# An attention and feed-forward block on one core: LayerNorm's normalisation and most of its reciprocal roots on GpSimd, GpSimd's additions without a window, and new build parameters and seeds

## The chip, the cores and the metric

The kernel runs on one core of a Trainium2 chip. The metric is the device time of one execution in microseconds; 2048 rows, bfloat16 inputs and output, one launch. The engines are TensorE (PE in the profile; PEld is its weight load), ScalarE (ACT), VectorE (DVE), GpSimd (POOL) and SyncE (SP), which here issues all DMAs.

## The reference, cut to what matters

```python
S, D, H, Dh, F = 2048, 640, 32, 20, 1536
xn = (x - mean(x)) / sqrt(var(x) + 1e-5)          # LayerNorm without weights
q = xn @ wq                                       # 32 heads of 20
k, v = xn @ wk, xn @ wv                           # one head for K and V, shared by all
p = softmax(q @ k.T * Dh ** -0.5)                 # 2048 x 2048 for each head
attn = concat_heads(p @ v) @ wo
ffn = relu(xn @ w1 + b1) ** 2 @ w2 + b2
out = x + attn + ffn
```

## The kernel before, in words

**A planner writes the order.** The kernel has no loops on the chip. While it is built, a scheduler (class `Sched`, `run` from line 292) plays the whole program through in simulated time: each part of the work is a generator that yields a request (`Req`) with an engine, a planned duration, its dependencies and a priority; the scheduler takes for each engine the request that can start first (the lowest priority number among those within 15 ns) and appends it to that engine's list. The lists are then emitted in this order, with a semaphore wait wherever an instruction depends on another engine. Each engine runs its list strictly in order, so the plan fixes who stands behind whom. Planned durations and thresholds are constants of the file. `PLAN` is a table of 64 rows, one for each half block of the attention: thresholds and, in most rows, a `seed` that flips some of the planner's choices (`pick`). Other seeds give another order of the same work.

**The opening.** x is 16 tiles of 128 rows, in chunks of four. Chunk 0 takes a short cut that computes its Q, K and V from the raw x, so that the attention can begin early. For all tiles VectorE computes mean and variance (`stats`, L708 and L711). `rst` (line 716) makes the reciprocal root on ScalarE, as a logarithm and an exponential, for half a chunk at a time in chunk 0 and for a chunk at a time in chunks 1 to 3 (L717, L723). `nmean` (L733) makes -mean x root, and `xnorm` (L743) the normalised tile on VectorE: `x * rstd + nmr`, written into the buffer `big`. The normalised tile is then transposed into `xnT`: by TensorE with an eviction by VectorE for the tiles in `PET` = 5, 6, 7 (`u_T`, L951 and L905), by a DMA transpose that SyncE issues for all others (`turn`, L910). Chunk 0 is normalised last: `X0W` = 12 makes it wait for the transposes of tiles 4 to 11. From `xnT` follow K and V of chunks 1 to 3 (`u_KT`, `u_V`; evictions L986 and L1003; a cast of V on GpSimd, L1010), the Q projections (L1053 evicts them, L1071 spreads them by DMA into `qT`) and the feed-forward. W1's load (`weights`, L655) waits until all transposes are issued, and the feed-forward until all are done, because its buffer shares memory with the normalised tiles. TensorE fills gaps of the opening with useless matmuls to keep its clock up (L1813, L1815).

**The attention** has 32 blocks (4 chunks of 512 queries x 8 groups of 4 heads), each with 16 tiles of 128 keys. Scores are computed transposed (keys on partitions, 512 queries): four heads can run at once in four row strips of TensorE, and a batch (L1318) has two, three or four of them. Each tile of keys has one of two ways:

- *A tile*: ScalarE's exponential (L1595) takes two or three heads in one instruction from adjacent PSUM banks (banks 0, 1, 2 or banks 3, 4) into one of `RING` slots. P x V is one group of four matmuls (L1896, `PT,vx`).
- *D tile*: VectorE makes the exponential from the bits of the scores: one eviction per head (L1694, `S_P1`) into one of `NPB` buffers, and then three shifted copies, the phases, which are additions of a constant to 128 x 2048 16-bit integers: on VectorE (L1715, `S_PH` and `S_STEAL`) or on GpSimd as 64-bit additions (L1777, `S_PHP`). P x V takes four groups (`pbx,vx` once, `pbx,vp` three times). Scores of D heads go to banks 5, 6, 7, which P x V and all other work share, or to bank 2 when the planner takes it from a three-head exponential: it does so when VectorE has less planned work left than `W32` ns (`poll_s`, line 1376).

`DPH` is the share of phases that VectorE takes at once; the rest go into a queue for GpSimd, out of which VectorE takes one when the queue is longer than `PHQ`.

**VectorE and GpSimd take turns.** Requests with `port=True` (VectorE's normalisation, phases L1715, squares L1106, products L1957) and all of GpSimd's work are planned so as not to overlap. GpSimd's phase additions are `under=True`: the planner puts them only beneath a VectorE instruction of at least 550 ns that is no port operation (`beneath`, line 386), and cuts them into pieces that fit there (`cut`, `pieces`). A GpSimd piece waits for the last port operation of VectorE; VectorE's port operations have no wait on GpSimd.

**The end.** The output of a tile half (128 rows x 320 columns) is W2's 12 groups of four matmuls plus Wo's six (L962). In the last chunk `u_P1` does W2's part and the ready Wo groups early and keeps the sum in SBUF (L1220), and `u_PF` does the missing Wo groups at the end, added by VectorE (L1156). `NPX` = 1 tile (two halves) is done wholly at the end by `u_PX`, and evicted by VectorE or ScalarE as a copy (L1153, L1154). The last block is normalised by `norm_last` (L1977 to L1989) on VectorE, in two halves.

## Time and profile before

| what | value |
|---|---|
| median of 3 runs | 679.76 us (679.63 to 681.91) |
| the profiled execution | 681.03 us, its span 679.3 us |
| granted clock of TensorE | 0.997 |
| instructions | 23577 |
| first and last exponential (L1595) start at | 10.9 and 669.3 us |
| DMA transposes of normalised tiles (L910) | 13 |
| D tiles (matmuls `pbx,vx` 620 / 4) | 155 of 512 |

The span runs from the first to the last instruction of that execution. Busy time of TensorE counts overlapping matmuls once, and their ends are modelled. In an order of time an instruction's line shows its start, its length, the engine, the line of the program and, in brackets, how long the engine was idle before it and who released it. L962 and L1896 are lines of helpers that many parts use; there the names of the tiles tell the parts apart.

### The profile page before, as it was taken

Reading aid. Unit: us, or ns where it says so; the run is one execution under the profiler, and the core shown is the slowest. Engines: PE = TensorE matmul, PEld = TensorE weight load, DVE = VectorE, ACT = ScalarE, POOL = GpSimd, SP = SyncE. Lnnn points to the kernel's source line nnn. Section 1 sums busy time; section 2 is a strip of 40 time slices with the busy share of each in tenths; the row PEclk is TensorE's granted clock in tenths of the full one; section 3 lists DMA queues with packets and bytes.
Section 4 is the critical chain, followed back from the end, with each engine's and each line's share of the span. In section 5 each row is a group of like instructions: output and inputs, shape, how many; then the busy total and the mean of one; then the engine's idle time right before and its main releaser. Section 6 shows DMA issues by size and latency. Waiting matters only on the chain.

```text
span 679.3 us, 23577 instructions
## 1 busy us (share of the span) xinstructions
PE 668.8 (98%) x9953; PEld 226.4 (33%) x9953; DVE 607.0 (89%) x1097; ACT 659.5 (97%) x664; POOL 452.2 (67%) x827
## 2 busy tenths in 40 slices
PE   8999999999999999999999999999999999999998
PEld 5322222233223333332223333333222333333434
DVE  7978999999999998989999888888999899997895
ACT  6989999999999999999999999999999999999995
POOL 2073775787577866777778886786666877687700
PEclk9989999999999999999999999999999999999999
DMA  7282244111110111111000112111110011111001
GB/s 222 51 145 76 56 113 102 29 22 28 30 21 16 43 42 23 47 42 26 20 20 18 28 46 46 26 34 42 30 25 18 20 39 37 32 42 47 12 2 41
DMA packets 39891, 29.90 MB, mean 44 GB/s; under 512 B 23562, under 2 KB 34795, under 8 KB 39787
## 3 DMA queue, kind: packets, MB, share of 16 engines
q1 hardware_dynamic: 39787, 28.39, 18.0%
q8 instruction: 80, 1.31, 0.8%
q14 instruction: 24, 0.20, 0.1%
HBM read 11.12 MB, written 2.62 MB: 20 GB/s over the span
## 4 chain that ended last, share of the span: by engine, by line
PE 64%; ACT 33%; DVE 2%; DMA 1%; issue 0%; POOL 0%; DVEq 0%
ACT PT L1595 32%; PE ps L1896 25%; PE ps L1318 20%; PE ps L962 19%; DMA xnT<-big 1%; DVE pbx L1694 1%; DMA pbx<-in_A_x_dram 0%; DVE stats L708 0%; PE ps L999 0%; DVE out_sb L1156 0%; PE ps L1813 0%; DVE OTs L1957 0%; DVE pbx L1715 0%; POOL pbx L1777 0%; DVE mv L711 0%
## 5 line engine op out<-in xcount | busy, mean ns | idle before, releaser
L1595 ACT ACTIVATE PT<-ps 128x1024 bf16<-128x1024 f32 (+1 forms) x642 | 653.0, 1189 | 7.1 <-PE ps L1318 6.7
L1777 POOL INT64_ADD pbx<-pbx x803 | 447.3, 576 | 171.4 <-DVE pbx L1715 74.9
L1694 DVE TENSOR_SCALAR pbx<-ps 128x512 int16<-128x512 f32 x619 | 407.0, 684 | 49.9 <-PE ps L1318 45.9
L1318 PE MATMUL ps<-qT,kT 20*128 20x512 bf16 x2048 | 250.0, 385 | 2.5 <-ACT PT L1595 2.2
L1896 PE MATMUL ps<-pbx,vp 128*32 128x512 bf16 x1860 | 169.7, 383 | 0.2
L1318 PEld LDWEIGHTS ps<-qT,kT 20*128 20x128 bf16 x2048 | 62.6, 91 | 242.4 <-ACT PT L1595 164.8
L1896 PE MATMUL ps<-PT,vx 128*32 128x512 bf16 x1428 | 136.2, 384 | 0.4 <-ACT PT L1595 0.3
L962 PE MATMUL ps<-w_sb,big 128*32 128x320 bf16 x1536 | 74.7, 302 | 0.0
L962 PE MATMUL ps<-xnT,w_sb 128*32 128x512 bf16 x960 | 73.7, 383 | 0.1
L1715 DVE TENSOR_SCALAR pbx<-pbx 128x2048 int16<-128x2048 int16 x98 | 66.5, 691 | 0.5
L1896 PEld LDWEIGHTS ps<-pbx,vp 128*32 128x32 bf16 x1860 | 45.5, 95 | 51.6 <-issue 30.6
L1896 PE MATMUL ps<-pbx,vx 128*32 128x512 bf16 x620 | 60.5, 385 | 0.1
L1896 PEld LDWEIGHTS ps<-PT,vx 128*32 128x32 bf16 x1428 | 36.1, 95 | 43.9 <-issue 31.4
L962 PEld LDWEIGHTS ps<-w_sb,big 128*32 128x32 bf16 x1536 | 32.7, 95 | 28.4 <-issue 22.0
L1098 DVE TENSOR_SCALAR hT_tmp<-ps,b1col 128x512 bf16<-128x512 f32 x48 | 35.6, 742 | 1.2 <-PE ps L962 0.9
L962 PE MATMUL ps<-wo_p,OTp 120*32 120x320 bf16 (+1 forms) x640 | 31.8, 301 | 0.1
L962 PE MATMUL ps<-xnT,wq_sb 128*32 128x512 bf16 x375 | 28.5, 383 | 0.0
L962 PEld LDWEIGHTS ps<-xnT,w_sb 128*32 128x32 bf16 x960 | 18.6, 95 | 27.3 <-issue 17.7
L1896 PEld LDWEIGHTS ps<-pbx,vx 128*32 128x32 bf16 x620 | 16.2, 95 | 18.7 <-issue 12.0
L1941 DVE COPY Tn<-ps 128x512 f32<-128x512 f32 x29 | 19.8, 682 | 0.5 <-PE ps L1896 0.5
L1106 DVE TENSOR_TENSOR big<-hT_tmp 128x512 bf16<-128x512 bf16 x48 | 20.2, 425 | 0.0
L962 PEld LDWEIGHTS ps<-wo_p,OTp 120*32 120x32 bf16 (+1 forms) x640 | 14.7, 95 | 11.6 <-issue 4.7
(95 smaller groups left out, 188.9 us busy)
## 6 DMA issues: line engine op xcount, KB each, us to landing
Rb<-kT SPq DMA_DIRECT2D x29, 256.0 KB
xres<-in_A_x_dram SPq DMA_DIRECT2D x16, 160.0 KB
out_dram<-out_sb SPq DMA_DIRECT2D x16, 160.0 KB
qT<-qpk SPq DMA_DIRECT2D x105, 20.0 KB
pbx<-in_A_x_dram SPq DMA_DIRECT2D x3, 640.0 KB
w_sb<-in_B_w_dram SPq DMA_DIRECT2D x1, 1920.0 KB
w_sb<-in_B_w_dram SPq DMA_DIRECT2D x4, 480.0 KB
OTp<-OTs SPq DMA_DIRECT2D x96, 20.0 KB
```

The costliest lines, as they stand in the source:

```text
L962: return lambda e: e.matmul(ps[32 * j:32 * j + m, b_[0], 0:n], Lj, R, start=first, stop=last, tile_position=(0, 32 * j))
L1098: v = yield Req(("dve", 658.0, 742.0, [lambda e: e.tensor_scalar(out=hT_tmp[:, k, :], in0=ps[:, b_[0], :], scalar1=b1col[:, f:f + 1], scal ...
L1106: w = yield Req(("dve", SQ_D, SQ_D + 82.0, [lambda e: e.tensor_tensor(out=h2T[:, qc % 2, f, :], in0=hT_tmp[:, k, :], in1=hT_tmp[:, k, :], ...
L1318: ins.append(lambda e, i=i, b=b, t=t, h=h: e.matmul(ps[:, i, :], kT[32 * h:32 * h + DH, t * 128:(t + 1) * 128], qT[32 * h:32 * h + DH, b % ...
L1595: op = yield Req(("act", d_, d_ + 107.0, [lambda e, slot=slot, n=n, src=src: e.activation(out=PT[:, slot:slot + n, :], in_=ps[:, src, :], ...
L1694: return Req(("dve", d_, d_ + 82.0, [lambda e: e.tensor_scalar(out=PB[:, k, hsl, :], in0=ps[:, bk:bk + np_, :], scalar1=OFFS, scalar2=0.0, ...
L1715: return Req(("dve", 600.0, 684.0, [lambda e: e.tensor_scalar(out=PB[:, k, :, :], in0=PB[:, s, :, :], scalar1=PH_D[j], scalar2=None, op0=A ...
L1777: return lambda e: e.int64_add(PB8[:, k, c0 // 4:c1 // 4], PB8[:, s, c0 // 4:c1 // 4], int(PH_D[j]) * 0x0001000100010001)
L1896: ins = [(lambda e, h=h, first=first, last=last: e.matmul(ps[32 * h:32 * h + 32, bk, :], lhs, rhs[h], start=first, stop=last, tile_positio ...
L1941: v = yield Req(("dve", 600.0, 682.0, [lambda e: e.tensor_copy(out=Tn[:, tb, :], in_=ps[:, pvb, :])]), (lambda: None if oldt() is None els ...
```

## The change

- **Normalisation and roots.** GpSimd loads library 0 behind its memsets, and library 1 (with the 64-bit addition) again when all 16 tiles are normalised; no phase addition is planned on GpSimd before that. All 16 normalisations are GpSimd's (`XPOOL`). For tiles 4 to 15 GpSimd also makes the reciprocal root, tile by tile: `var + EPS`, then that to the power -0.5, and the normalisation is `(x - mean) * rstd`. Chunk 0 keeps ScalarE's roots.
- **Transposes.** `PET` becomes 4, 5, 6, 7, 11. `X0W` = 0: chunk 0 is normalised as soon as it may; its transposes are planned after tile 11 is normalised. DMA transposes come first among what SyncE may issue.
- **GpSimd's additions** (`PUN` = False) are planned at any time, whole, and no longer beneath a VectorE instruction. Where a port operation of VectorE and a GpSimd addition or normalisation follow each other, the later waits for the earlier, in both directions.
- **Parameters**: `RING` 25 to 23, `NPB` 10 to 11, `NQS` (slots of `qT`) 6 to 4; in nearly all rows of `PLAN` `W32` 2000 to 650, `DPH` 0.3 to 0, `PHQ` 4 to 8; other seeds.
- **The end**: `NPX` = 0, all eight halves of the last chunk go through `u_P1` and `u_PF`; `PAT` 27.6 to 26.5 (the block at which `u_P1` begins); `u_PF` may begin before `u_P1`'s eviction, its groups but the last have priority 0.6 and the last one -1.
- The other lines (`spot`, `where`, `pvres`, the condition in `PVblk`) leave the planner's choices as they were with the constants given (`PVK` = 1, `PVS` = 1, `PVG` = 0).

```diff
-RING = 25
-NPB = 10
+RING = 23
+NPB = 11
...
-NQS = 6
+NQS = 4
...
-PAT = 27.6
+PAT = 26.5
...
-    (640, 3500.0, 600.0, 6000.0, 0, 900.0, 12, 2, 0.0, 3, 60.0, 600, 4.0, 2000.0, 2, 0.3, 0, 0.0, 0.0, 4, 0.5, 2, (0, 3, 400.0, 300.0), 1, 0, 8, 1.0, 2.0, 2, 99, 2000.0, -1, 400.0, 600.0),
...
+    (640, 3500.0, 600.0, 6000.0, 0, 900.0, 12, 2, 0.0, 3, 60.0, 600, 4.0, 650.0, 2, 0.0, 0, 0.0, 0.0, 8, 0.5, 2, (0, 3, 400.0, 300.0), 1, 0, 8, 1.0, 2.0, 2, 99, 2000.0, -1, 400.0, 600.0),
...
-NPX = 1
+NPX = 0
+PUN = False
+PFA, PFB, PFE = 0.6, -1.0, 0
+PVK, PVR, PVS, PVG = 1, 16, 1, 0
...
-PET = (5, 6, 7)
+PET = (4, 5, 6, 7, 11)
...
-XPOOL = ()
-X0W = 12
+XPOOL, VPOOL, LIBD = (0, 1, 2, 3, 4, 5, 6, 7, 8, 9, 10, 11, 12, 13, 14, 15), (), 5800.0
+GPW, PWD = 1, 130.0
+XG, TG = '', 'X11'
+TEDP = -1
+X0W = 0
...
+            if not PUN and self.last_port is not None and (eng == "pool" and rr.name == "PHP" or rr.port) and self.last_port.eng != eng:
+                deps = deps + [self.last_port]
...
-            if eng == "dve" and rr.port:
+            if rr.port or not PUN and rr.name == "PHP":
                 self.last_port = op
...
+            if XPOOL:
+                done["mhalf"] = yield ms(mhalf[:], -0.5, 100.0, "mhalf")
+                done["lib0"] = yield Req(("pool", 7850.0, 7850.0, [lambda e: e.load_library(library_config.all_libraries[0])]), [], -2, "lib0")
+                yield Until(lambda: have(*[f"X{st}" for st in XPOOL]) and (not VPOOL or have(*[f"VP{c}" for c in VPOOL])))
+                done["lib1"] = yield Req(("pool", LIBD, LIBD, [lambda e: e.load_library(library_config.all_libraries[1])]), [], -2, "lib1")
...
+        def rpow(st):
+            yield Until(lambda: have("lib0"))
+            v = yield (lambda: Req(("pool", PWD, PWD + 60.0, [lambda e: e.tensor_scalar(out=vtmp[:, st:st + 1], in0=mv[:, st, 1:2], scalar1=EPS, scalar2=None, op0=ALU.add)]),
+                                   (lambda: get(f"S{st}")), soon(st) - 0.3, f"RV{st}"))
+            op = yield (lambda: Req(("pool", PWD, PWD + 60.0, [lambda e: e.tensor_tensor(out=rstd[:, st:st + 1], in0=vtmp[:, st:st + 1], in1=mhalf[:, :], op=ALU.pow)]),
+                                    (lambda: get("mhalf") + [v]), soon(st) - 0.4, f"RW{st}"))
+            done[f"RW{st}"] = op
...
             if st in XPOOL:
-                alts = [("pool", 700.0, 760.0, alts[0][3])]
+                alts = [("pool", 870.0, 930.0, alts[0][3])]
+            if st in XPOOL:
+                yield Until(lambda: have("lib0"))
+            if GPW and c:
+                eng, d_, l_ = ("pool", 870.0, 930.0) if st in XPOOL else ("dve", 400.0, 440.0)
+                alts = [(eng, d_, l_, [lambda e: e.tensor_scalar(out=xn_sb[:, st, :], in0=x_sb[:, st, :], scalar1=mv[:, st, 0:1], scalar2=rstd[:, st:st + 1], op0=ALU.subtract, op1=ALU.mult)])]
+                yield Until(lambda: have(f"RW{st}"))
...
-            yield Until(lambda: f"X{st}" in done)
+            yield Until(lambda: f"X{st}" in done and (st > 3 or not TG or TG in done))
...
                 def poll():
+                    if XPOOL and "lib1" not in done:
+                        return None
...
-                    c1 = cut(2048, F_, E_)
+                    c1 = cut(2048, F_, E_) if PUN else 2048
...
-                    return Req(("pool", d_, d_ + 60.0, [part(0, c1, k, s, j)]), [acc[-1]] + pbres[k].last, 2 if left_ns(b) > PHU else -1, "PHP", under=True)
+                    return Req(("pool", d_, d_ + 60.0, [part(0, c1, k, s, j)]), [acc[-1]] + pbres[k].last, 2 if left_ns(b) > PHU else -1, "PHP", under=PUN)
```

## The prediction

> **What bounds the kernel now.** I read the page's totals first, then the table by stage, then the instructions in order of time for the stages that are not full, then the groups by shape for durations. Columns of the stage table: stage, its length, busy time of PE, PEld, DVE, ACT and POOL, granted clock, DMA share, GB/s.
>
> ```profile
> PE 668.8 (98%) x9953; PEld 226.4 (33%) x9953; DVE 607.0 (89%) x1097; ACT 659.5 (97%) x664; POOL 452.2 (67%) x827
> ```
> ```profile
> 20.00:30.00 10.00, 8.74 (x121) 3.06 (x123) 9.82 (x34) 9.14 (x12) 0.25 (x1) 1.00 0.17 34
> 30.00:40.00 10.00, 9.70 (x134) 2.89 (x126) 9.85 (x28) 9.16 (x12) 4.53 (x10) 1.00 0.61 101
> 40.00:60.00 20.00, 18.69 (x227) 5.29 (x223) 12.69 (x23) 17.58 (x20) 13.77 (x29) 0.91 0.63 139
> 60.00:100.00 40.00, 40.00 (x526) 11.09 (x526) 39.67 (x71) 40.00 (x44) 25.16 (x42) 1.00 0.30 77
> 500.00:600.00 100.00, 99.98 (x1523) 32.85 (x1520) 91.93 (x156) 99.92 (x101) 72.43 (x131) 1.00 0.13 30
> 670.00:680.00 10.00, 5.91 (x164) 3.98 (x156) 5.43 (x15) 0.85 (x2) 0.00 (x0) 0.93 0.21 69
> ```
>
> From 60 us to the last exponential ScalarE and TensorE are both full; VectorE and GpSimd are not. So a saving on VectorE or GpSimd there is worth nothing by itself. It pays only where it lets TensorE or ScalarE do less, and those two are coupled: a tile taken from ScalarE goes to VectorE and costs TensorE three more groups. What is visibly unused lies in the opening. Its ScalarE, its transposes and the chain of waits:
>
> ```profile
> 27.05 5.12 ACT L1595 ACTIVATE PT<-ps 128x1536 bf16<-128x1536 f32 x5 [0.83 <-PE ps L1318]
> ...
> 38.66 9.21 ACT L1595 ACTIVATE PT<-ps 128x1536 bf16<-128x1536 f32 x9 [0.84 <-PE ps L1318]
> 49.73 1.02 ACT L1595 ACTIVATE PT<-ps 128x1024 bf16<-128x1024 f32 x1 [1.86 <-PE ps L1318]
> 51.24 11.72 ACT L1595 ACTIVATE PT<-ps 128x1024 bf16<-128x1024 f32 x12 [0.48 <-PE ps L1318]
> ```
> ```profile
> 26.71 9.77 SPq L910 DMA_TRANSPOSE xnT<-big  x6
> ```
> ```profile
> 35.21 10.50 SPq L910 DMA_TRANSPOSE xnT<-big  x7
> 45.75 0.59 SPq L655 DMA_DIRECT2D w_sb<-in_B_w_dram  x1
> ```
> ```profile
> 41.82 5.03 DMA xnT<-big
> ```
>
> Each ScalarE gap (bracket: length, releaser) ends with a scores batch that had to wait for the next chunk of K: chunk 1 before 27, chunk 2 before 38.7, chunk 3 before 49.7. Together 0.83 + 0.84 + 1.86 + 0.48 = 4.0 us. The last chunk waits for SyncE's transposes: 12 of them, one behind the other, from 26.71 to 45.75, 1.59 us each; the chain shows that transfer for 5.03 us. W1's load is queued behind them, at 45.75.
>
> **The change, part by part.** Durations are those of one profiled execution: span 679.3, 681.03 with the 1.73 us around it, which is 1.27 above the median of 679.76. I subtract savings from the median.
>
> *Normalisation and roots off VectorE and ScalarE.*
>
> ```profile
> L717 ACT ACTIVATE vtmp<-mv 128x4 f32<-128x4 f32 x3 | 0.7, 248 | 0.0
> L723 ACT ACTIVATE rstd<-vtmp 128x4 f32<-128x4 f32 x3 | 0.6, 216 | 0.0
> L672 POOL MEMSET wo_p<- 128x640 bf16 x1 | 0.6, 631 | 0.0
> L1813 PE MATMUL ps<-kT,zeros 128*32 128x512 bf16 x76 | 6.8, 385 | 0.0
> ```
> ```profile
> L743 DVE TENSOR_SCALAR big<-pbx,rstd,nmr x16: 431/439/445, 17.4 to 36.8; 128x640 bf16<-128x640 bf16 x16
> ```
> ```profile
> 16.67 0.25 POOL L1010 CAST vx<-out_sb 128x80 bf16<-128x80 f32 x1 [11.93 <-DVE out_sb L824]
> ```
>
> VectorE loses 16 x 0.439 = 7.0 us, ScalarE six small operations, 1.3 us. GpSimd gets 16 normalisations and 12 pairs of tiny operations. No row has a GpSimd normalisation; the nearest is its 128x640 memset, 0.63 us, which reads nothing. The planner charges 0.87 and 0.13 for a tiny one, and I take those: 16 x 0.87 + 24 x 0.13 = 17 us. They fit: GpSimd is idle for 11.93 us before 16.67, and the first library load (planned at 7.85) lies in that hole, ending near 12.6 if it starts at 4.8. Tiles 4 to 7 are then normalised by 12.6 + 4 x 1.13 = 17.1, while VectorE only begins them at 17.4 now. For tiles 8 to 15 the statistics, not GpSimd, set the pace. I reckon the last normalisation near 31 (the last starts at 36.8 now) and, after the second load of 5.8, GpSimd's first addition near 38 (33.2 now, below). That delay costs nothing as long as VectorE's shares wait in buffers.
>
> The Trainium skill (GPSIMD Engine Reference, When to use GPSIMD) says that ordinary elementwise work belongs on the Vector engine, GpSimd being about half as fast for two inputs and near line rate for one. By it the move is a loss of engine time, and 0.439 against 0.63 or more agrees; but the loss falls on an idle engine. The same page (Architecture, Instruction dispatch) gives about 6 us, with no visible instruction, for the first call into a freshly loaded library. Two of them would make 12 where the planner has 13.65, so the sum would not move. No run so far shows it.
>
> *Transposes.* Tiles 4 and 11 move from SyncE to TensorE, X0W = 0 lets chunk 0 be normalised early, and chunk 3 no longer queues at the end of a full line. 11 x 1.59 = 17.5 us of transposes starting near 19, with holes, end near 38 instead of 45.75. K3 then comes near 42 (38 and the 4.0 from 45.75 to 49.73), before ScalarE needs it at 49.73 - 1.86 - 0.83 - 0.84 = 46.2, and W1's load goes out near 38, eight us earlier. So I remove the four gaps (4.0) and the roots (1.3): **ScalarE gains 5.3 us**, bounds 0 and 5.3.
>
> TensorE has to gain as well. In the opening it runs 19 filler groups (76 / 4) of 0.22, 4.1 us, idles 1.26 + 0.30 + 1.31 between 20 and 60, and loses 20 x 0.09 = 1.8 to the clock of 0.91 after the stall: 8.8 in all. Only what starts before W1 arrives can fill it (the Q projections of chunk 0, then the feed-forward): **I take 5**, bounds 0 and 8.8.
>
> *How two slacks become time.* A tile costs ScalarE 4 x 0.457 = 1.83 us (653.0 over the 498 x 2 + 144 x 3 = 1428 heads below). Given to VectorE it costs TensorE three groups of 0.22, 0.65 us. If ScalarE has A and TensorE S to spare, both end together when the time falls by 0.26 A + 0.74 S. So 0.26 x 5.3 + 0.74 x 5 = **5.1 us**.
>
> *Additions at any time, new parameters and seeds.*
>
> ```profile
> L1595 ACT ACTIVATE PT<-ps 128x1024 bf16<-128x1024 f32 x498 | 482.0, 1096 | 5.3 <-PE ps L1318 5.0
> L1777 POOL INT64_ADD pbx<-pbx x803 | 447.3, 576 | 171.4 <-DVE pbx L1715 74.9 <-DVE big L1106 30.2 <-DVE pbx L1694 23.7
> L1595 ACT ACTIVATE PT<-ps 128x1536 bf16<-128x1536 f32 x144 | 216.6, 1513 | 1.8 <-PE ps L1318 1.7
> L1896 PE MATMUL ps<-pbx,vp 128*32 128x512 bf16 x1860 | 169.7, 383 | 0.2
> L1715 DVE TENSOR_SCALAR pbx<-pbx 128x2048 int16<-128x2048 int16 x98 | 66.5, 691 | 0.5
> ```
> ```profile
> L1777 POOL INT64_ADD pbx<-pbx x803: 263/572/1048, 33.2 to 645.6; - x161
> ```
> ```profile
> L1595 ACT ACTIVATE PT<-ps 128x1024 bf16<-128x1024 f32 (+1 forms) x642 | 653.0, 1189 | 7.1 <-PE ps L1318 6.7
> ```
>
> There are 1860 / 4 = 465 phase additions: 98 on VectorE, 367 on GpSimd in 803 pieces, 1.22 us each. Whole they should cost the longest piece, 1.048 (second row: min, median, max). All 465 on GpSimd take 487 us of the 612 between 38 and 650: they fit. VectorE sheds up to 66.5. The price is mutual exclusion: about 77 remaining port operations of VectorE (48 squares, 29 normalisations of the output) wait up to 1.05 for an addition, half on average, 40 us. Behind one in VectorE's queue stand the evictions that free the PSUM banks of the scores. VectorE has 72 us idle plus the 66.5, so it has cover; I cost this at nothing, and at 40 us of VectorE without cover.
>
> What can pay is the scores batch. TensorE's order of time shows its price:
>
> ```profile
> 657.03 0.40 PE L1896 MATMUL ps<-pbx,vp 128*32 128x512 bf16 x4
> 657.25 0.39 PE L1896 MATMUL ps<-PT,vx 128*32 128x512 bf16 x4
> ...
> 658.40 0.39 PE L1318 MATMUL ps<-qT,kT 20*128 20x512 bf16 x3
> 658.72 0.73 PE L962 MATMUL ps<-w_sb,big 128*32 128x320 bf16 x16
> 659.38 0.39 PE L1318 MATMUL ps<-qT,kT 20*128 20x512 bf16 x3
> 659.70 0.59 PE L962 MATMUL ps<-w_sb,big 128*32 128x320 bf16 x12
> 660.22 0.39 PE L1318 MATMUL ps<-qT,kT 20*128 20x512 bf16 x3
> ```
>
> A group of four 512-column matmuls takes 0.22 (657.03 to 657.25), one of 320 columns 0.14 (0.66 less 0.52), so a batch with its two changes of mode takes 0.98 - 4 x 0.14 = 0.43 us, whether two, three or four heads ride in it. Each exponential has a batch, so 642. W32 falls from 2000 to 650: bank 2 is taken from a three-head exponential only when VectorE has less work left, which favours threes. But VectorE's counted work falls too, as no phases wait in it, and that favours twos. Neither end can be excluded: 680 batches (10% threes) to 621 (30%). I take 10 fewer, since VectorE's relief frees the banks sooner: 4.3 us of TensorE, x 0.74 = **3.2 us**. RING, NPB and NQS trade the same memory; I cost them at nothing while Q lands in time.
>
> *The end.*
>
> ```profile
> 670.83 1.80 PE L962 MATMUL ps<-w_sb,big 128*32 128x320 bf16 x48
> ```
> ```profile
> 672.50 0.77 DVE L1989 STREAM_TRANSPOSE OT<-qpk 128x256 bf16<-128x256 bf16 x2
> 673.50 0.49 DVE L1153 CAST out_sb<-ps 128x320 bf16<-128x320 f32 x1 [0.24 <-PE ps L962]
> 674.19 2.65 DVE L1156 TENSOR_TENSOR out_sb<-ps,w_sb 128x320 bf16<-128x320 f32 x6 [0.19 <-PE ps L962]
> ```
>
> NPX = 0 takes the 12 groups at 670.83 out of the shadow of VectorE's last normalisation and puts them into the full stretch: 1.8 x 0.74 = 1.3 lost. PF's early groups now fill the shadow and the eight additions start at once, but all eight are VectorE's: 8 x 0.44 = 3.5 from about 673.1 ends at 676.6, against 674.19 + 2.65 = 676.84 now, 0.2 back. **Net 1.1 us slower.**
>
> **Sum:** 5.1 + 3.2 - 1.1 = 7.2; 679.76 - 7.2 = **672.6 us**.
>
> **Rivals.** *Only the opening pays*: batches stay at 642; 679.76 - 5.1 + 1.1 = 675.8. For it: W32 and the counted work cancel. *Threes become common*: 621 batches, 21 x 0.43 x 0.74 = 6.7; 679.76 - 5.1 + 1.1 - 6.7 = 669.1. *The opening's gain doesn't come*: the loads take longer than planned, or the casts of V (the row at 16.67 is one) stand behind the second load and the ring of 23 fills; K1, due at 27.05 - 0.83 = 26.2 and reckoned near 21 (17.1 and some 4 for a transpose, its eviction, the projection and K's eviction), has 5 us of margin, and past it each us is lost on both engines. Then 3.2 - 1.1 remain, less a us or two: 679. *Fewer threes (slower)*: VectorE, relieved, asks for scores more often, takes bank 2, and the exponentials fall to pairs. Each batch more is two threes less and costs 0.32 us; the opening and the end give 4.0, so it decides from 642 + 13 = 655 batches (118 threes). At 668 (92 threes): 26 x 0.32 - 4.0 = 4.3 slower, 684.1. Against it: ScalarE's bank 2 was already contested at W32 = 2000.
>
> **How the numbers follow.** Forecast 0.45, only the opening 0.20, common threes 0.12, no opening gain 0.10, fewer threes 0.13. A measurement here tells about 0.5%, 3.4 us, from no change. Faster than 676.4: the forecast, the common threes and three quarters of the second case, 0.72; within: 0.13; slower: 0.15. The range, 665 to 684, takes in TensorE's whole slack of 8.8 beside common threes (669.1 less 0.74 x 3.8 = 666.3) at one end and the slower case's middle at the other.
>
> **What would show it.** As expected: no ScalarE gap over 0.5 us between 20 and 52, W1's issue before 40, TensorE's filler groups halved, the longest addition and the mean one both near 1.05, fewer than 642 exponentials.
>
> ```profile
> PEld ps L1896 <- POOL pbx L1777: 6.5, 25, 0.5
> ```
>
> Wrong: a ScalarE gap behind chunk 1 of K (library), more than 655 exponentials, TensorE waiting for GpSimd's additions (6.5 us in 25 waits now, row above), or VectorE's evictions late behind port operations.

## The result, and the profile after

The kernel after takes 707.9 us (707.2 to 712.7, 4 executions) against 680.1 us for the kernel before on the same chip: ratio 1.042 [1.037, 1.047], slower. The profiled execution took 708.4 us, its span is 706.6 us.

The page's totals and its row of granted clock (40 slices of 17.7 us):

```profile
PE 686.4 (97%) x9964; PEld 229.1 (32%) x9964; DVE 576.5 (82%) x1013; ACT 654.7 (93%) x651; POOL 519.1 (73%) x527
...
PEclk9555799999999999999999999999999999999999
```

The table by stage (columns as in the prediction):

```profile
20.00:30.00 10.00, 5.30 (x39) 2.21 (x43) 2.80 (x9) 3.02 (x4) 9.99 (x10) 0.55 0.00 0
30.00:40.00 10.00, 9.73 (x83) 2.10 (x75) 6.24 (x21) 6.86 (x7) 10.00 (x10) 0.50 0.18 35
40.00:60.00 20.00, 16.32 (x130) 3.65 (x130) 8.92 (x21) 11.18 (x12) 17.53 (x17) 0.50 0.47 75
60.00:100.00 40.00, 39.97 (x422) 9.63 (x418) 24.79 (x45) 32.74 (x35) 22.41 (x23) 0.76 0.24 76
500.00:600.00 100.00, 99.79 (x1435) 30.68 (x1435) 89.45 (x151) 99.88 (x99) 77.43 (x76) 1.00 0.13 27
```

GpSimd, nearly idle in the opening before (0.25 of 10 us from 20 to 30), is now the full engine to 58 us; ScalarE is busy for 30, 69 and 56% of the first three stages, against 91, 92 and 88% before; and TensorE runs at half its clock from 21 to 79 us. From 100 to 600 us nothing has become slower. How far behind the kernel is can be read by counting the score matmuls up to 100 us and from there to 600 (some records may be missing). Before, then after:

```profile
0.00:100.00 100.00, 33.76 (x251) 8.37 (x251) 0.98 0.46 112
100.00:600.00 500.00, 192.04 (x1596) 48.26 (x1596) 1.00 0.15 33
```
```profile
0.00:100.00 100.00, 30.66 (x165) 6.17 (x165) 0.71 0.34 87
100.00:600.00 500.00, 192.12 (x1614) 48.37 (x1611) 1.00 0.15 35
```

It is 86 matmuls behind at 100 us; at 1596 / 500 = 3.19 a us that is 27 us, the whole difference of the spans (27.3). So the loss is made in the opening. (From 100 to 600 us it does 18 score matmuls more than before; what that lead is worth is seen below, in e14.) GpSimd's groups by shape:

```profile
L777 POOL TENSOR_SCALAR big<-pbx,mv,rstd 128x640 bf16<-128x640 bf16 x12 | 30.1, 2514 | 0.1
L747 POOL TENSOR_TENSOR rstd<-vtmp,mhalf 128x1 f32<-128x1 f32 x12 | 6.7, 562 | 0.1
L770 POOL TENSOR_SCALAR big<-pbx,rstd,nmr 128x640 bf16<-128x640 bf16 x4 | 3.5, 876 | 0.0
L745 POOL TENSOR_SCALAR vtmp<-mv 128x1 f32<-128x1 f32 x12 | 2.6, 225 | 9.8 <-DVE mv L725 9.8
```

The four tiles of chunk 0 (L770, multiply and add) take 0.876 us each, as planned. The twelve others (L777, subtract and multiply) take 2.51, the power 0.56 and var + EPS 0.23: 3.3 us a tile where 1.13 was planned. The 9.8 us idle before L745 is the first library load: the statistics of the first tile that it waits for are there at 12.76 us, and GpSimd begins at 14.56. Then GpSimd's first addition, and TensorE's waits in order of time:

```profile
64.23 6.11 POOL L1824 INT64_ADD pbx<-pbx  x6 [6.51 <-DVE pbx L1741]
```
```profile
18.95 0.44 PE L984 MATMUL ps<-ident,big 128*128 128x128 bf16 x5 [1.75 <-POOL big L777]
22.29 0.62 PE L1947 MATMUL ps<-PT,vx 128*32 128x512 bf16 x4 [2.90 <-POOL vx L1043]
...
28.14 1.22 PE L984 MATMUL ps<-ident,big 128*128 128x128 bf16 x10 [2.40 <-POOL big L777]
...
43.68 0.69 PE L984 MATMUL ps<-ident,big 128*128 128x128 bf16 x5 [3.95 <-POOL big L777]
```

TensorE waits 11 us for GpSimd: for tile 4, for the cast of V (queued behind two normalisations), for tiles 7 and 11. The first addition starts at 64.2 in place of 33.2.

### The profile page after: what moved, and what is told of

The parts are those of the page before. It is cut to its first block, busy times and chain, and to the rows that moved or that the text cites. A ratio compares the mean times of both kernels' runs of the same rounds, so it can differ in the third digit from the quotient of the medians.

```text
span 706.6 us, 23246 instructions
## 1 busy us (share of the span) xinstructions
PE 686.4 (97%) x9964; PEld 229.1 (32%) x9964; DVE 576.5 (82%) x1013; ACT 654.7 (93%) x651; POOL 519.1 (73%) x527
## 3 DMA queue, kind: packets, MB, share of 16 engines
HBM read 11.12 MB, written 2.62 MB: 19 GB/s over the span
## 4 chain that ended last, share of the span: by engine, by line
PE 75%; POOL 15%; DVE 7%; issue 1%; DMA 1%; ACT 0%
PE ps L1947 29%; PE ps L1362 24%; PE ps L995 23%; POOL pbx L1824 11%; POOL big L777 3%; DVE pbx L1741 3%; DVE big L1139 1%; DVE hT_tmp L1131 1%; DVE stats L722 1%; POOL rstd L747 1%; DVE OTs L2008 1%; DMA pbx<-in_A_x_dram 0%; POOL big L770 0%; DVE pbx L1762 0%; DMA dn<-Tn 0%
## 5 line engine op out<-in xcount | busy, mean ns | idle before, releaser
L1824 POOL INT64_ADD pbx<-pbx x462 | 471.8, 1041 | 134.5 <-DVE pbx L1741 64.8
L1741 DVE TENSOR_SCALAR pbx<-ps 128x512 int16<-128x512 f32 (+1 forms) x629 | 421.0, 694 | 77.5 <-PE ps L1362 72.0
L1362 PE MATMUL ps<-qT,kT 20*128 20x512 bf16 x2048 | 255.3, 393 | 2.1 <-DVE pbx L1741 1.3
L1947 PE MATMUL ps<-pbx,vp 128*32 128x512 bf16 x1920 | 175.2, 386 | 0.1
L995 PE MATMUL ps<-w_sb,big 128*32 128x320 bf16 x1536 | 71.2, 301 | 0.0
L1947 PEld LDWEIGHTS ps<-pbx,vp 128*32 128x32 bf16 x1920 | 47.0, 95 | 53.6 <-issue 33.3
L1947 PE MATMUL ps<-pbx,vx 128*32 128x512 bf16 x640 | 63.2, 387 | 0.5 <-DVE pbx L1741 0.5
L995 PE MATMUL ps<-xnT,wq_sb 128*32 128x512 bf16 x375 | 30.9, 408 | 0.0
L777 POOL TENSOR_SCALAR big<-pbx,mv,rstd 128x640 bf16<-128x640 bf16 x12 | 30.1, 2514 | 0.1
```

The lines of the kernel that those rows point to most:

```text
L777: alts = [(eng, d_, l_, [lambda e: e.tensor_scalar(out=xn_sb[:, st, :], in0=x_sb[:, st, :], scalar1=mv[:, st, 0:1], scalar2=rstd[:, st:st ...
L995: return lambda e: e.matmul(ps[32 * j:32 * j + m, b_[0], 0:n], Lj, R, start=first, stop=last, tile_position=(0, 32 * j))
L1362: ins.append(lambda e, i=i, b=b, t=t, h=h: e.matmul(ps[:, i, :], kT[32 * h:32 * h + DH, t * 128:(t + 1) * 128], qT[32 * h:32 * h + DH, b % ...
L1741: return Req(("dve", d_, d_ + 82.0, [lambda e: e.tensor_scalar(out=PB[:, k, hsl, :], in0=ps[:, bk:bk + np_, :], scalar1=OFFS, scalar2=0.0, ...
L1824: return lambda e: e.int64_add(PB8[:, k, c0 // 4:c1 // 4], PB8[:, s, c0 // 4:c1 // 4], int(PH_D[j]) * 0x0001000100010001)
L1947: ins = [(lambda e, h=h, first=first, last=last: e.matmul(ps[32 * h:32 * h + 32, bk, :], lhs, rhs[h], start=first, stop=last, tile_positio ...
```

## The experiments

Two things could cost the 27 us: GpSimd's chain being late, or TensorE's clock at half for 58 us. They had to be told apart. A third possibility is that the other parts of the change (additions at any time, seeds, the new end) lose by themselves. A ratio is to the kernel before on the same chip. Useless matmuls are added after the planner has run, so that the order of everything else stays: `EXTRA["pe", k, 0]` holds what TensorE does ahead of entry k of its list, `early` is one useless matmul of 256 columns, and `zeros_at(k, n)` puts n groups of four 512-column matmuls with zeros there. The code cuts show the main lines of an edit; `...` stands for what is left out.

### What GpSimd's operations cost

**e4_forms**: the kernel before, with a list of operations behind its GpSimd work.

```diff
+            e.load_library(library_config.all_libraries[0])
...
+                for s1, s2, o0, o1 in ((m1, r1, ALU.subtract, ALU.mult), (r1, n1, ALU.mult, ALU.add), (m1, None, ALU.subtract, None), (n1, r1, ALU.add, ALU.mult),
+                                       ...
+                    e.tensor_scalar(out=big_(), in0=xi, scalar1=s1, scalar2=s2, op0=o0, ...)
...
+                    e.tensor_tensor(out=tiny(k), in0=rstd[:, 0:k], in1=rstd[:, 4:4 + k], op=ALU.pow)
```

> The kernel before with a list of GpSimd instructions behind its last addition (results unused): library 0 loaded, then twice: seven forms of a two-operation instruction on 128x640 bf16 (subtract and multiply with column operands; multiply and add; subtract alone; add and multiply; multiply and subtract; subtract and multiply with constants; multiply and add with constants), powers and products of 1, 4 and 12 columns, and the tiny factor. Theory 1: about 2.5 us for subtract-multiply, 0.88 for multiply-add; open which of operation, order and operand makes the difference. Power: 0.56 for one column; if its cost is per instruction, 12 columns cost nearly the same. Load of the library: 6 to 10 us.

GpSimd in order of time, second pass (subtract and multiply; multiply and add; subtract alone; add and multiply; power of 1 and of 4 columns):

```profile
675.91 2.50 POOL L2174 TENSOR_SCALAR xnT<-wq_sb,mv,rstd 128x640 bf16<-128x640 bf16 x1
678.39 0.88 POOL L2174 TENSOR_SCALAR xnT<-wq_sb,rstd,nmr 128x640 bf16<-128x640 bf16 x1
679.25 1.89 POOL L2174 TENSOR_SCALAR xnT<-wq_sb,mv 128x640 bf16<-128x640 bf16 x1
681.12 0.88 POOL L2174 TENSOR_SCALAR xnT<-wq_sb,nmr,rstd 128x640 bf16<-128x640 bf16 x1
...
687.47 0.58 POOL L2176 TENSOR_TENSOR stats<-rstd 128x1 f32<-128x1 f32 x1
...
688.16 1.03 POOL L2176 TENSOR_TENSOR stats<-rstd 128x4 f32<-128x4 f32 x1
```

A subtraction is what is slow: 1.89 us alone (2.31 in the first pass) and 2.50 with a second operation, where an addition and a multiplication together take 0.88 in either order.

**e1_mult_add**, **e2_no_pow**, **e3_thrice**: the plan and order of the kernel after; the normalisation of tiles 4 to 15 as x * root + (-mean * root); then also a product for the power (the reciprocal root is left out); then, with the power again, the fast form three times over.

```diff
-... e.tensor_scalar(out=xn_sb[:, st, :], in0=x_sb[:, st, :], scalar1=mv[:, st, 0:1], scalar2=rstd[:, st:st + 1], op0=ALU.subtract, op1=ALU.mult) ...
+... e.tensor_scalar(out=nmr[:, st:st + 1], in0=mv[:, st, 0:1], scalar1=rstd[:, st:st + 1], scalar2=-1.0, op0=ALU.mult, op1=ALU.mult) ...
+... e.tensor_scalar(out=xn_sb[:, st, :], in0=x_sb[:, st, :], scalar1=rstd[:, st:st + 1], scalar2=nmr[:, st:st + 1], op0=ALU.mult, op1=ALU.add)
```

> The changed kernel with the plan of every engine unchanged; only GpSimd's 12 normalisations of tiles 4 to 15 are written as x * root + (-mean * root), with a tiny instruction for the last factor, in place of (x - mean) * root. Theory 1, the form of the normalisation costs the time (2.51 us each in the changed kernel's profile, 0.88 in the form that its tiles 0 to 3 have): each tile gets 2.51 - 0.88 - 0.23 = 1.4 us shorter, the last one ends near 41 instead of 57.7, TensorE's clock stays up most of the time, 678 to 690 us. Rival 1, additions at any time, parameters and seeds cost it: over 700, with GpSimd's opening shorter all the same. Rival 2, the two library loads cost it: over 700 and the gap of some 9.8 us before GpSimd's first root stays.

> As the one before, and GpSimd's 12 powers (0.56 us each) replaced by a multiplication of one column (about 0.22): the kernel leaves the reciprocal root of tiles 4 to 15 out. Plan unchanged. Theory 1: 4 us less in GpSimd's opening, last normalisation near 37, 674 to 684 us, that is near or under the kernel before. Rival 1: over 700. Rival 2: over 700.

> The fast form again, but each of the 12 normalisations done three times (two into unused columns): 3 x 0.88 + 0.23 = 2.87 us in place of 2.51, plan unchanged. Theory 1 says that it is GpSimd's time and nothing else about the slow form: 708 to 718 us, the clock down to half again from about 20 us on. If the slow form hurt in another way (a port that it holds, VectorE's or the transposes' slowness beside it): clearly under 700.

Measured 699.3 (1.028 [1.027, 1.030]), 701.9 (1.032 [1.026, 1.038]) and 725.6 us (1.067 [1.065, 1.069]). The slow form is worth 8.6 us, less than expected, and a GpSimd chain that is shorter still (e2) brings nothing more. What goes with e1 and e2 is the clock. e1 by stages:

```profile
25.00:30.00 5.00, 5.00 (x52) 1.35 (x49) 4.26 (x15) 2.49 (x3) 4.48 (x10) 0.50 0.18 38
...
60.00:65.00 5.00, 5.00 (x55) 1.36 (x47) 2.06 (x6) 3.34 (x4) 0.28 (x1) 0.50 0.03 7
65.00:70.00 5.00, 5.00 (x48) 1.08 (x48) 2.36 (x4) 3.58 (x5) 3.06 (x3) 0.63 0.00 0
70.00:75.00 5.00, 5.00 (x71) 1.21 (x64) 3.72 (x7) 4.99 (x6) 3.09 (x3) 1.00 0.02 3
```

TensorE is busy without a gap from 25 us on and yet stays at 0.50 for 40 us: 39 to 55 matmuls in 5 us, against 71 at full clock. My first theory, the slow form alone, fell here.

### The clock

**e5_fill_gap**, **e6_burst**: e1 with useless matmuls in TensorE's first two pauses (ahead of tile 4's transposes and of the first P x V), or with one dense piece of them behind these pauses.

```diff
+        EXTRA["pe", 51, 0], EXTRA["pe", 52, 0] = [early] * 11, [early] * 16
```
```diff
+        EXTRA["pe", 64, 0] = zero * 8
```

> The kernel of e1_mult_add (699.3 us), with 11 useless 256-column matmuls more on TensorE ahead of tile 4's transposes and 16 more ahead of the first P x V, where TensorE waited 1.26 and 1.83 us (17.07 to 18.34 and 18.78 to 20.61). GpSimd's work is not touched. Theory A (the clock): the granted clock fell to 0.5 at about 21 us because TensorE paused, and stayed there to about 67 us; without the pause it stays at 1.0 and the time falls by half of most of that stretch: 677 to 685 us, with 0.9 or more granted from 20 to 65 us. Theory B (the length of GpSimd's opening work costs the time, the clock only goes with it): GpSimd's last normalisation still ends near 44 us, so the time stays at 697 to 701 us.

> The kernel of e1_mult_add, the pause left as it is, with eight groups of four useless 512-column matmuls (zeros added to the first block's sum) in one piece on TensorE ahead of the matmuls of V of chunk 1, near 27 us, when the clock has been at half for some 5 us. Theory A with a sharper reading (the clock comes back when TensorE's work is dense for a few us, which the alternation of two-head score batches with single groups at half clock doesn't reach): the clock is back at 1.0 near 32 us in place of 67, and the time is 680 to 690 us, the burst itself costing up to 4. Theory A without it (the clock comes back after a time of its own, 45 us or more): 699 to 704 us, half clock to beyond 60 us. Theory B: 699 to 703 us.

Measured 700.4 (1.031 [1.027, 1.034]) and 696.6 us (1.024 [1.021, 1.027]). In e5 the clock held to the next pause, and fell 1.1 us behind its end, at 24.7:

```profile
23.54 0.72 PE L997 MATMUL ps<-ident,big 128*128 128x128 bf16 x10 [1.39 <-POOL big L774]
```
```profile
20.00:25.00 5.00, 3.61 (x45) 1.57 (x43) 1.87 (x6) 3.23 (x4) 4.57 (x10) 0.97 0.01 3
25.00:30.00 5.00, 5.00 (x55) 1.41 (x50) 3.48 (x13) 3.47 (x4) 4.54 (x10) 0.50 0.17 34
```

In e6 the clock came back, and fell again 1.4 us behind the next pause (1.30 us, tile 11, ending at 35.3). But the dense piece is not what brought it back:

```profile
25.90 0.83 PE L1960 MATMUL ps<-PT,vx 128*32 128x512 bf16 x8
26.56 1.90 PE L2202 MATMUL ps<-kT,zeros 128*32 128x512 bf16 x32
```

Two groups take 0.62 us at full clock and 1.04 at half, so the 0.83 at 25.90 hold the change, and the eight groups of the piece (1.90 us) ran at full clock from the start; windows of 0.2 us put the return at 26.4. What e6 shows is the second fall. By stages:

```profile
25.00:30.00 5.00, 5.00 (x79) 2.13 (x76) 3.39 (x12) 1.61 (x2) 4.48 (x9) 0.86 0.18 38
30.00:35.00 5.00, 3.96 (x45) 1.14 (x43) 3.99 (x12) 5.00 (x6) 4.62 (x10) 1.00 0.33 66
35.00:40.00 5.00, 4.71 (x55) 1.70 (x55) 2.83 (x7) 3.44 (x5) 4.61 (x12) 0.66 1.01 128
```

That a dense piece does bring it back is seen in three later runs: e18 (2.78 us of zeros from 47.30, back at 49.1), e10 (2.62 us from 56.84, back at 59.2) and e9, where it came 1.4 us behind the piece's end:

```profile
46.33 2.78 PE L2209 MATMUL ps<-kT,zeros 128*32 128x512 bf16 x24
49.04 0.61 PE L1375 MATMUL ps<-qT,kT 20*128 20x512 bf16 x3
...
50.55 0.39 PE L1375 MATMUL ps<-qT,kT 20*128 20x512 bf16 x2
```

Groups of four in alternation with score batches, at half clock, brought it back too, but at very different times: 7 us after the fall in e6, 48 in e1. Nor does the length of a pause decide a fall: 1.39 us in e5 was followed by one, 1.37 us in e10 wasn't:

```profile
28.55 0.72 PE L988 MATMUL ps<-ident,big 128*128 128x128 bf16 x10 [1.37 <-POOL big L781]
```
```profile
30.00:35.00 5.00, 5.00 (x75) 1.89 (x71) 4.85 (x19) 4.56 (x6) 5.00 (x6) 1.00 0.17 34
```

The Trainium skill (TensorE: Matmul & The Clock Gate, Part 1) gives an idle window of some 3.4 us for the fall and some 3.4 us of sustained work for the return. It also notes, in a warning that the clock events of a trace can be unreliable, a clock seen stuck low for over 50 us. The dense pieces of e9, e10 and e18, with the clock back 1.8 to 4.3 us after they began, are near the return; but a pause of 1.39 us sufficed for the fall, and in e1 40 us without an idle slice did not bring the return, which is nearer to the note than to the rule. The matmuls bear the record out (a score batch takes 0.39 us at full clock, 0.61 at half). The measurement decides.

One regularity runs through all the profiles: every stretch at half clock is a whole number of times 3.41 us long, read by windows of 0.25 us. It is 3.42 us in the kernel before, 6.84 in e6's first, 13.66 in e9, 17.07 in e10, 30.72 in e18's first, 47.78 in e1, 58.04 in the kernel after and 64.85 in e13: 1, 2, 4, 5, 9, 14, 17 and 19 times. That reads as if the clock were decided once in each 3.41 us, so that it matters where in such a step a pause falls; what is counted within a step, no run here isolates.

**e7_late_cast**, **e8_late_cast_fill**, **e15_before_fill**: the kernel before, with the cast of chunk 0's V 5 us late; the same with TensorE's wait filled; and the kernel before with its own pause at 46.1 us filled.

```diff
+                e.memset(big[:, 10240:11840], 0.0).then_inc(sx, 1)
+        EXTRA["pool", 17, 1] = [late]
```
```diff
+        EXTRA["pe", 50, 0] = [early] * 48
```
```diff
+        zeros_at(139, 4)
```

> The kernel before (679.8 us), with three useless memsets of 128x1600 (some 5 us) on GpSimd ahead of the cast of chunk 0's V alone; nothing else is changed. The first P x V then starts near 22 us in place of 17.0, and TensorE pauses for 5 us, as it does after the change. Theory A: the clock falls to half there and stays there for tens of us: 692 to 710 us. Theory B (only the wait itself): 680 to 686 us, the 5 us less what slack takes.

> The kernel of e7_late_cast, the same 5 us late, with 48 useless 256-column matmuls (5.1 us) on TensorE ahead of the first P x V, so that it works through the wait. Theory A: the clock stays at 1.0, and what is left is the wait itself: 681 to 687 us, and at least 8 us less than e7_late_cast. Theory B: the same as e7_late_cast within 2 us.

> The kernel before with four groups of useless matmuls (0.9 us) where TensorE waits 0.88 us for a transpose's DMA at 46.1 us, behind which the granted clock is 0.92 and 0.50 in the stretches 45 to 47.5 and 47.5 to 50 us. If a pause of that length is what lowers the clock: 1.0 through 45 to 52.5 us, and 1 to 2 us less than the kernel before (677.5 to 679). If it has another cause: 679.5 to 680.5 us and the same clock.

Measured 685.7 (1.009 [1.008, 1.011]), 683.2 (1.005 [1.004, 1.007]) and 679.3 us (0.9995 [0.9987, 1.0004]). The clock did as the theory has it: 0.50 in 20 to 25 us in e7 and 1.00 in e8. But in the kernel before's order it was back at 25.9, behind three groups of P x V, one of zeros and fifteen transposes; e7 lies in the range of theory B, and the filling saved 2.4 us, not 8. In e15 the clock was 1.00 in all twelve executions (679.0 to 679.6 us), and the median did not move, because most executions of the kernel before don't have the fall. Of the 71 that were taken beside these experiments, 13 have a mean clock of 0.996 or 0.997 and take 681.1 us on average, the 58 others 679.6. So a fall of one step of 3.4 us costs some 1.5 us where it comes, and filling the pause took it away. The prices I had expected for the clock were too high.

**e9_fill_all**, **e10_fill_all_after**: every wait of TensorE for GpSimd filled over the length that it had, in e1 and in the kernel after.

```diff
+        EXTRA["pe", 51, 0], EXTRA["pe", 52, 0] = [early] * 11, [early] * 16
+        for k, n in ((59, 6), (82, 6), (89, 2), (105, 6), (129, 6)):
+            zeros_at(k, n)
```
```diff
+        EXTRA["pe", 51, 0], EXTRA["pe", 52, 0] = [early] * 16, [early] * 27
+        for k, n in ((59, 11), (82, 18), (89, 2), (105, 6), (129, 6)):
+            zeros_at(k, n)
```

> e5_fill_gap filled only the first pause, and the clock fell some 2 us behind the next one (1.39 us at 22.2, for tile 7's normalisation); in e6_burst 1.9 us of dense work brought it back, and the next pause (1.30 us at 34, tile 11) took it again. So here every wait of TensorE of the kernel of e1_mult_add (699.3 us) that is due to GpSimd is filled with useless matmuls: 11 and 16 as in e5_fill_gap, six groups of zeros ahead of the transposes of tile 7 and of tile 11, two ahead of V of chunk 2, and six each ahead of chunk 0's Q and of chunk 3's K. GpSimd is not touched. Theory A (the clock): granted clock 0.9 or more from 20 to 65 us, and what remains over the kernel before is the waits themselves, some 5.8 us, less the some 3 us that the rest of the change gains: 679 to 687 us. Theory B (GpSimd's length): 697 to 702 us.

> The same filling in the kernel after itself (708 us), with its slow normalisations: 16 and 27 useless matmuls for the waits of 1.75 and 2.90 us, 11 groups of zeros for the 2.40 us ahead of tile 7's transposes, 18 for the 3.95 us ahead of tile 11's, and two, six and six as in e9_fill_all. TensorE's waits for GpSimd add up to 11 us and stay. Theory A: the clock holds at 0.9 or more to 45 us at least, and the time is 680 + 11 - 3 = 688, so 685 to 695 us; of the 28 us that the change lost, some 17 are then the clock's and 11 the waits'. Theory B: 704 to 710 us.

Measured 694.1 (1.021 [1.019, 1.024]) and 705.4 us (1.038 [1.035, 1.041]): 5 and 3 us less, not the 12 to 20 and 13 to 23 of theory A. At full clock TensorE ran into the next wait sooner: tile 11's transposes came at 34.8 and 44.1 us, about where they come without the filling (35.6 and 43.7), and it waited 2.51 and 4.54 us for them on top of the filling. Behind these waits the clock fell again, from 36.9 to 50.6 and from 42.1 to 59.2 us.

**e18_one_burst** shows the same at a later place: the kernel after, with one dense piece behind its last long pause.

```diff
+        zeros_at(89, 8)
```

> The kernel after itself (707.9 us), with nothing else than eight groups of four useless matmuls in one piece on TensorE ahead of V of chunk 2, near 47.5 us: behind its last long pause (3.95 us, ending at 43.7), where it is busy without a gap and yet stays at half clock to 78 us. Theory A (dense work brings the clock back, the ordinary alternation at half clock doesn't): 1.0 from some 51 us on in place of 78; half of those 27 us less the 2.5 us of the burst, so 11 us less: 694 to 700 us, and the rest of the 28 us, some 17, are TensorE's waits for GpSimd and the half clock before. Without that mechanism: 707 to 711 us.

Measured 706.9 us in four executions (706.5 to 707.4), 1.0400 [1.0385, 1.0415], and 722 in two more at a lower mean clock (0.945 against 0.968): no gain to speak of, though in the profiled execution the clock came back at 49.1. By stages, and TensorE at 64 us:

```profile
50.00:55.00 5.00, 5.00 (x80) 1.78 (x76) 3.33 (x11) 3.96 (x5) 4.84 (x5) 1.00 0.38 49
55.00:60.00 5.00, 5.00 (x66) 1.31 (x67) 2.87 (x5) 5.00 (x6) 2.51 (x1) 1.00 0.34 67
60.00:65.00 5.00, 1.61 (x21) 0.38 (x19) 1.29 (x2) 2.21 (x3) 1.48 (x2) 0.78 0.95 333
65.00:70.00 5.00, 4.60 (x35) 0.76 (x31) 0.69 (x1) 2.21 (x3) 4.62 (x5) 0.50 0.28 96
```
```profile
64.60 0.62 PE L1951 MATMUL ps<-pbx,vp 128*32 128x512 bf16 x4 [3.38 <-POOL pbx L1828]
```

At full clock TensorE reaches the first P x V of a D tile early, and waits for GpSimd's first addition, which stands behind the second library load. This wait then lowers the clock once more, from 62.8 to 76.4 us. So between 49 and 64 us of the kernel after the clock isn't what bounds: half clock only hides the wait for GpSimd. e10 says the same of the whole opening: with 17 us at half clock in place of 58 it is 3 us faster.

### The change at the prices of its plan

**e11_plan_prices**, **e13_plan_prices2**, **e14_plan_prices_fill**, **e16_plan_prices_end**: a product for the power and x * var + mean, with library 0 loaded first (e11); with the load in its place (e13); with TensorE's short waits filled as well (e14); and with the old end's share and start (e16; `NPX` counts halves since the change, so 2 is the one tile of before).

```diff
-... op=ALU.pow ...
+... e.tensor_scalar(out=rstd[:, st:st + 1], in0=vtmp[:, st:st + 1], scalar1=1.0, scalar2=None, op0=ALU.mult) ...
-... scalar1=mv[:, st, 0:1], scalar2=rstd[:, st:st + 1], op0=ALU.subtract, op1=ALU.mult ...
+... scalar1=rstd[:, st:st + 1], scalar2=mv[:, st, 0:1], op0=ALU.mult, op1=ALU.add ...
```
```diff
+        EXTRA["pe", 52, 0] = [early] * 8
+        for k, n in ((59, 2), (82, 5), (105, 4), (129, 4)):
+            zeros_at(k, n)
```
```diff
-PAT = 26.5
+PAT = 27.6
-NPX = 0
+NPX = 2
```

> The change at about the prices that its plan was made with: the kernel after the change, its plan, order and waits untouched, but the power is replaced by a product (so the reciprocal root is left out), the normalisation by x * var + mean (0.88 us in place of 2.5), and library 0 is loaded at the very start in place of library 1, where no GpSimd work is held up, so that the 9.8 us hole goes. A tile then costs GpSimd 0.22 + 0.20 + 0.88 = 1.3 us against 1.13 planned. Theory C (the whole loss comes from GpSimd's opening work taking longer than planned, first by TensorE's waits for it, then by the clock that these waits lower): TensorE's waits for GpSimd stay under 1 us, granted clock 0.95 or more in 15 to 60 us, last normalisation at 31 to 36 us, and the time is 672 to 681 us, 27 to 36 less than the kernel after. Theory D (the additions at any time, the new seeds or the new end lose by themselves): 690 us or more.

> e11_plan_prices showed that library 0 loaded first holds up GpSimd's own memsets to 9.4 us, and with them the whole opening by 8.5 us; its times (686.6 to 706.9 us) are that much too long. Here the load stays where the change put it (4.8 to 14.5 us), and the rest is as in e11_plan_prices: a product in place of the power (the reciprocal root is left out) and x * var + mean in 0.88 us, 1.3 us a tile. Theory C (GpSimd's opening work alone sinks the change, by TensorE's waits and the clock that they lower): 673 to 682 us where the clock holds, with some 8 us more in executions in which it falls behind one of the short waits that are left (V of chunk 0 about 1 us late, tile 11). Theory D (additions at any time, seeds or end lose by themselves): 690 us or more, with the clock at 1.0 too.

> The kernel of e13_plan_prices2 with useless matmuls on TensorE where it would still wait: 8 of 256 columns ahead of the first P x V, two groups of zeros ahead of tile 7's transposes, five ahead of tile 11's, four each ahead of chunk 0's Q and chunk 3's K. Theory C: the granted clock holds at 0.95 or more from 15 to 70 us, and the time is 673 to 680 us in all executions, below the kernel before. Theory D: 690 us or more.

> The kernel of e14_plan_prices_fill (681.7 us; product for the power, x * var + mean) with the end of the kernel before: its last tile is done wholly at the end, and the early output units begin at block 27.6. e14 was 12 score matmuls (3.7 us) ahead of the kernel before at 600 us and ended level with it; its last exponential ends at 662.9 us, and 17.1 us follow it, against 8.9 in the kernel before. If the new end loses by itself: 676 to 679.5 us. If its output work is only moved from the attention to the end, with TensorE full either way: 681 to 684 us.

e11 took 699.0 us (686.6 to 706.9) and doesn't answer the question: library 0 loaded first holds GpSimd's own memsets, and so the first matmul, up to 9.4 us. e13's four executions took 682.5, 695.9, 698.3 and 704.7 us, in the order of their mean clocks (0.995, 0.970, 0.965, 0.954): the same kernel. In the profiled one, the slowest, the clock fell behind a wait of 1.09 us for the cast of V and stayed at 0.50 to 85 us:

```profile
18.77 0.40 PE L1947 MATMUL ps<-PT,vx 128*32 128x512 bf16 x4 [1.09 <-POOL vx L1043]
```
```profile
25.00:30.00 5.00, 5.00 (x36) 0.89 (x34) 2.69 (x8) 3.47 (x4) 4.78 (x9) 0.50 0.66 95
```

With the waits filled (e14) it holds at 1.00 in the whole span, and the time is 681.7 us, 1.0045 [1.0026, 1.0063]. So GpSimd's prices and the clock together account for 26 of the 28 us. The other parts, with both library loads in place, lose no more than the 2 to 3 us that are left; of these, some belong to what e14 still has over the plan (1.3 us a tile against 1.13, a first load of 10.0 us against 7.85). Taken together the other parts gain nothing either. e14's score matmuls, and the matmuls of W2 from 600 us on, in the kernel before and in e14:

```profile
0.00:100.00 100.00, 34.79 (x253) 8.76 (x253) 1.00 0.42 108
100.00:600.00 500.00, 191.03 (x1610) 48.13 (x1610) 1.00 0.15 33
```
```profile
L962 PE MATMUL ps<-w_sb,big 128*32 128x320 bf16 x384 | 17.6, 301 | 0.0
```
```profile
L999 PE MATMUL ps<-w_sb,big 128*32 128x320 bf16 x528 | 22.6, 300 | 0.0
```

At 100 us e14 is level (253 against 251). To 600 it gets 14 score matmuls ahead, 4.4 us, and has 144 matmuls of W2 more to do afterwards: 5.0 us of TensorE's time (22.6 less 17.6). The lead was borrowed. e16, with the old end's share, took 682.8 us, 1.0037 [1.0024, 1.0050], the same.

**e12_load_first**, **e17_grouped_roots**: the whole computation. e12 is e1 with library 0 loaded first and its later load left out. e17 makes the roots of four tiles, then of pairs, in one group of small instructions, normalises by multiply and add, and fills TensorE's waits as e14 does.

```diff
-e.load_library(library_config.all_libraries[1])
+e.load_library(library_config.all_libraries[0])
```
```diff
+        for a, b in ((4, 8), (8, 10), (10, 12), (12, 14), (14, 16)):
+            lead = pool[f"RV{a}"]
+            lead.ins, lead.deps = [roots(a, b)], lead.deps + pool[f"RW{a}"].deps + [das[f"DA{b - 1}"]]
```

> The kernel of e1_mult_add (699.3 us; nothing of the computation is left out) with library 0 loaded at the very start in place of library 1, and the later load of library 0 left out. GpSimd can begin its roots when the first statistics are there (12.5 us) in place of 15.1, and each tile still costs it some 2.0 us. Theory C: GpSimd runs 2 us less late at tile 4 and tile 7, TensorE's first waits shrink from 1.26 and 1.83 us to under 0.5 each, later ones remain, since 2.0 us a tile is 0.9 more than planned; 684 to 695 us. If the load's hole doesn't matter: 698 to 701 us.

> The whole computation, in the order of the kernel after, with cheaper operations: the roots of tiles 4 to 7 in one group of four small instructions on four columns, those of 8, 9 / 10, 11 / 12, 13 / 14, 15 in pairs, the normalisation as x * root + (-mean * root) in 0.88 us, and useless matmuls as in e14 (12 in place of 8 ahead of the first P x V). GpSimd then needs some 1.4 us a tile against 3.4 in the kernel after and 1.13 planned. Theory C (with prices near the plan and the clock held the change is level with the kernel before): granted clock 0.95 or more from 15 to 70 us, 681 to 686 us, 22 to 27 us less than the kernel after. If the clock still falls for long: 690 to 703 us.

e12: 716.4 us, 1.049 [1.041, 1.056], with the same 8.9 us late start as e11 and the clock at half from 29 to 101 us. e17: 688.8 us (686.2 to 689.7), 1.011 [1.009, 1.013]: 19 us less than the kernel after, by operations and filling alone. Its profile, with 1.00 granted in every slice, is of its fastest execution, 686.2 us; the three slowest have a mean clock of 0.995. The median is 3 us above the range that I expected; its first addition starts at 46.65, e14's at 42.0. What e17's operations give without the filling was not run.

First addition and half clock are read from the profiled execution, so its time stands beside the median.

| kernel | first addition, us | half clock, us | profiled, us | median, us |
|---|---|---|---|---|
| before | 33.2 | 47 to 51 | 681.0 | 679.8 |
| e14 (prices about as planned, waits filled) | 42.0 | none | 681.7 | 681.7 |
| e13 (prices about as planned) | 45.2 | 20 to 85 | 704.7 | 697.1 (682.5 to 704.7) |
| e17 (whole computation, cheap, waits filled) | 46.7 | none | 686.2 | 688.8 |
| e2 (fast form, no root) | 47.2 | 21 to 86 | 705.9 | 701.9 |
| e9 (e1, waits filled) | 50.0 | 37 to 51 | 693.9 | 694.1 |
| e1 (fast form) | 50.3 | 21 to 69 | 699.2 | 699.3 |
| after | 64.2 | 21 to 79 | 708.4 | 707.9 |
| e10 (after, waits filled) | 64.3 | 42 to 59 | 704.4 | 705.4 |
| e3 (fast form three times) | 70.5 | 20 to 108 | 724.8 | 725.6 |

Where the clock holds or nearly holds, the profiled time follows the first addition: 681.0, 681.7, 686.2, 693.9, 704.4 us for 33, 42, 47, 50, 64 us. This is an order of five kernels, not a test of the first addition by itself: all of GpSimd's opening work gets later with it, and only e18 shows TensorE standing for the addition. Where GpSimd is not late by more than some 17 us, a long stretch at half clock comes on top: 5 us in e1 against e9, 1 to 23 in e13's executions against e14. In the kernel after it adds 3 (against e10). So each of the two alone is enough for most of the loss, and they overlap.

## Why the prediction was wrong

- **The step that failed** is "No row has a GpSimd normalisation ... The planner charges 0.87 and 0.13 for a tiny one, and I take those: 16 x 0.87 + 24 x 0.13 = 17 us. They fit". Measured: 30.1 + 6.7 + 3.5 + 2.6 = 42.9 us (2.51 us for twelve of the normalisations, 0.56 for a power), and a first load of 9.8 us for the planned 7.85. The last normalisation ended at 57.7 us, not near 31, and the first addition started at 64.2, not 38. The memset's 0.63 us bounds such a cost from below only; I kept no upper end, so nothing of it reached the range.
- **"That delay costs nothing as long as VectorE's shares wait in buffers"** fell with it: in e18 TensorE, at full clock, stands 3.38 us for the first addition.
- **The clock had no term.** The prediction priced a fall once, as 1.8 us of slack in the kernel before. Where the fall comes it costs about that (1.5 us, beside e15), but the sum starts from a median that doesn't have it. And it did not ask what a new pause of TensorE would do to the clock: e13's executions lie between 682.5 and 704.7 us.
- **The opening's 5.1 us** do not come even at about the planned prices: e14 is level with the kernel before at 100 us. The four ScalarE gaps of 4.0 us in all were to go; e14 has seven others in their place between 18 and 49 us, of 0.16 to 1.11 us, 4.2 in all.
- **The batches' 3.2 us**: six fewer (636), not ten, and threes fell from 144 to 136. e14 shows the lead, and that it was W2's work put off.
- **The end's 1.1 us slower**: not seen; e14 and e16 differ by less than their intervals, but e16 has only the old share and start, not all of the old end.
- **Right**: additions take 1.04 us whole, and at any time they cost little: in e14 VectorE waits 9.0 us for them in all (40 without cover was the bound), TensorE 0.3; TensorE's planned fillers fell from 19 groups to 6; fewer than 642 exponentials.
- **The rival "the opening's gain doesn't come"** named the place: loads longer than planned, casts behind GpSimd's work, K1's 5 us of margin, past which both engines lose. It was given 0.10 and 679 us; what was off is the size. It allowed a us or two past the margin; the last normalisation came 27 us later than reckoned. Of the chances, 0.13 for no visible change and 0.15 for slower are the wrong way round: the cases listed give 0.05 + 0.10 and 0.13.

The Trainium skill (GPSIMD Engine Reference, Architecture, Instruction dispatch) gives about 6 us for the first call into a fresh library. The second loads here agree (GpSimd is idle for 5.7 to 6.5 us before its first addition); the first took 9.8 us in the kernel after, and 8.9 at the very start (e12).

What stays open: why GpSimd is slow at subtracting; and what decides a fall, or ends a stretch at half clock without a dense piece: 7 us in e6 and e7, but 48, 58 and 65 in e1, the kernel after and e13.

## What to carry to other kernels

A cost that no row shows needs an upper end as well as a lower one, and the form of the operation counts: on GpSimd the same normalisation takes 0.88 us as x * a + b and 2.5 us with a subtraction. Where a plan is written with assumed prices, run it once at those prices (e14): that tells in one run whether the idea or the price is at fault. Filling an engine's wait with work that keeps its clock up pays only where the thing waited for is nearly there; else the engine reaches the same wait sooner.
